# The last group's output tiles stored by column halves, in an attention and MoE kernel on one Trainium2 core

## The chip, the cores and the metric

The kernel runs on one core of one Trainium2 chip. The metric is the device time of one execution, in microseconds. A core has five engines that run their own instruction streams in order: PE (TensorE, the matrix products), DVE (VectorE), ACT (ScalarE), POOL (GpSimd) and SP (SyncE, here used for DMA only). They wait for one another through semaphores. Data lie in SBUF; PE writes its products to PSUM, 128 partitions of eight banks, from which DVE or ACT copy them out. DMAs are issued by SP, ACT or POOL, each with a queue of its own.

## What is computed

The reference does two attentions and then a feed-forward layer, on 8 batches of 8 heads, 576 tokens and 64 columns of a head; p is a pack of 32 rows for each batch and head.

```python
def sm_attn(qq, kk, vv):
    s = scale * np.matmul(qq, kk.transpose(0, 1, 3, 2))
    s = s - np.max(s, axis=-1, keepdims=True)
    a = np.exp(s)
    a = a / (np.sum(a, axis=-1, keepdims=True) + 1e-09)
    return np.matmul(a, vv)
p_packed = sm_attn(p, k, v)
x = sm_attn(q, p_packed, p_packed)      # as 4608 tokens x 512
h = x @ w_in                            # 512 x 2048
r = np.maximum(h, 0.0)
out = (r * r) @ w_out                   # 2048 x 512
```

Inputs and the output are float32; the products inside are of bfloat16 with float32 sums. The output is 4608 x 512, 9.4 MB.

## The kernel before, in words

**Work and stages.** For each of the eight batches, the first attention's scores are made (`s1_mm`, L736, or `x1_mm`), their maximum taken (`s1_max`, L755), the exponential e (`s1_exp`, L763), its transposes on PE (`s1_tr`, L769, five into one PSUM bank for each of two halves of the heads), a copy of them out (`s1_out`, through `cast`, L609 on ACT or L611 on DVE), and the product with v (`pv_mm`, L783). The result pp is normed (`pp_norm`, L792), transposed (`ppT_mm`, L802) and copied to ppT (`ppT_out`). The packed rows are then multiplied by w_in first (`m_mm`, L813; the product is called M, and copied out by `m_out` or, for batch 0, in two halves by `m_half`), and the second attention's weights, called a, are multiplied by M (`f1_mm`, L887, or `fh_mm`, L915, for parts of the first two batches). Its relu (r_b) and square give gT (`f1_relu`, `f1_sq`, `fh_relu`, `fh_sq`), the transposed input of the last product.

**The last product.** The 36 output tiles are 128 tokens by 512 columns. Twelve are made plainly, by 16 products over 2048 (`f2_mm`, L941), copied to o_sb (`f2_out`) and stored (`store`, L953). One of them, tile 31 (called TZ), is made in column halves (`fz_mm`, L959, `fz_out`). The other 24 stand in six groups of four tiles, `GROUPS` = 2 to 7, each a 2 x 2 block matrix product by seven half-size products instead of eight: sums of w_out and gT (`w_sum`, L986, `g_sum`, L993), the products (`gp_mm`, L1008), and copies and additions (`g_copy`, `g_add`, L1028) into the four quadrants (i, j) of the group's output, where i is a pair of tiles and j a half of the columns. The pieces of these are called GC.0 to GC.6; GC.2 finishes quadrant (0, 0), GC.6 (0, 1), GC.4 (1, 1) and GC.5 (1, 0).

**What sets the order.** The work is cut into pieces, each with its engine or a choice of engines, a duration, what it needs, the units that it takes (PSUM banks or pairs of banks, buffers of r_b, tiles of o_sb) and those that it frees. `Plan.forward` walks through time and starts, whenever an engine is free, the ready piece of the best priority: a level from the code plus a number from the long table `TABLE`. The instructions are then emitted in that order, under `tc.manual_schedule()`, so that each engine's stream is that of the plan. The waits between engines are not written in the kernel: they are derived, when it is built, from which instruction reads or writes which tile.

**PSUM.** One tile, `ps` (L595), holds all eight banks. `half(n)` (L600) is a bank of it, `pair(u)` (L603) two neighbouring ones. Banks 0 to 5 are taken as three pairs or, for the transposes, PV and the first plain tiles, singly (4 and 5, with 6 and 7); the outputs of the last product use banks 6 and 7 later on.

**Stores around the change** (L1303 to L1312). A group's tile needs both column halves: i = 0 waits for GC.2 and GC.6, i = 1 for GC.4 and GC.5. The tiles of the last group (those past TZ) are stored in two pieces of 64 tokens by 512 columns, 128 KB each, on whichever of SP, ACT or POOL the plan finds first (`store_any`, L1272). Tile 31 is stored in four pieces of 64 KB.

Of the kernel before, what the change touches and what calls it, by code (L numbers as in the profile page):

```python
# [14 lines left out]
P = 128  # L15
# [26 lines left out]
class Plan:  # L42
# [185 lines left out]
TABLE = {'o': {'Lk.0.0i': -36.900503, 'Lk.0.1i': 0.41924, 'Lk.0.0': -16.56608, 'LP.0': 169.009326, 'Lk.0.1':  # L228
# [292 lines left out]
def kernel_impl(tc, q, k, v, p, w_in, w_out, out):  # L521
# [23 lines left out]
    with ExitStack() as ctx:  # L545
# [45 lines left out]
        o_sb = consts.tile([P, NO, NE], F32, name="o_sb")  # L591
        still = consts.tile([P, 4], BF16, name="still")
        zero = o_sb[:, 0, :P].bitcast(BF16)

        ps = psum.tile([P, 8, 512], F32, name="ps")  # L595

        V, A = nc.vector, nc.scalar
# [802 lines left out]
```

## Time and profile before

| | |
|---|---|
| median of 3 runs | 234.08 us |
| lowest and highest | 233.74 and 234.46 us |
| the profiled execution | 233.42 us |
| its span in the trace | 231.7 us |
| mean granted clock of PE | 0.994 |
| HBM read and written | 37.22 MB and 9.44 MB |

The span goes from the first to the last event that the profiler recorded for the core, and the execution's own time is a little longer. Busy time is that of an engine's computing instructions. Matmuls are pipelined, so that neighbours overlap. In the rows below, `PEld` is PE's loading of the stationary operand, `SPq` and `ACTq` are the queues on which those engines issue DMAs, L and a number is a line of the kernel, and `out<-in` names tiles without their buffer numbers. A bracket at the end of a row is the idle time of the engine just before, and what ended it.

### The profile page before, as it was taken

To read this page: it belongs to the slowest core of one execution; us is meant where nothing else is said; L and a number is where in the kernel's file an instruction comes from. 1 tells how busy PE (TensorE), PEld (TensorE's weight loads), DVE (VectorE), ACT (ScalarE), POOL (GpSimd) and SP (SyncE) were. 2 spreads that over 40 slices of the span, in tenths; PEclk is the share of its full clock that TensorE was granted. 3 is DMA by queue.
4 is the path that set the end of the run, shared out by engine and by line. 5 is a ranking of instruction groups with operands and counts; after the bars stand their busy time and mean duration, and the time that the engine had idled before them with its cause. 6 is when DMAs were issued, how large, how long until landed. Compare 5 with 4: busy or idle time off the path is not lost.

```text
span 231.7 us, 6374 instructions
## 1 busy us (share of the span) xinstructions
PE 220.0 (95%) x2613; PEld 160.0 (69%) x2630; DVE 199.4 (86%) x336; ACT 148.4 (64%) x243; POOL 60.5 (26%) x108
## 2 busy tenths in 40 slices
PE   8978899999999999999999999999999999999991
PEld 5655664456654476768777877787668888888880
DVE  3679978999989999999999899999999997958340
ACT  3324994268955899775997936859988988310100
POOL 9787646333243575640000000000000000000010
PEclk9999999999999999999999999999999999999997
DMA  7999999999999999999999659757041001515325
GB/s 235 188 161 180 184 204 205 203 193 251 241 229 223 223 219 195 158 148 126 177 193 166 135 94 207 149 83 172 0 96 43 4 0 35 113 36 114 70 52 174
DMA packets 46668, 34.06 MB, mean 147 GB/s; under 512 B 25376, under 2 KB 38368, under 8 KB 46640
## 3 DMA queue, kind: packets, MB, share of 16 engines
q0 software_dynamic: 19488, 18.09, 50.5%
q1 hardware_dynamic: 26304, 14.98, 31.4%
q10 hardware_dynamic: 848, 0.59, 0.9%
q8 instruction: 20, 0.33, 0.6%
q14 instruction: 8, 0.07, 0.1%
HBM read 37.22 MB, written 9.44 MB: 201 GB/s over the span
## 4 chain that ended last, share of the span: by engine, by line
PE 83%; DVE 6%; DMA 5%; POOL 1%; issue 1%; ACT 1%; DVEq 0%; ACTq 0%; POOLq 0%
PE ps L1008 32%; PE ps L887 21%; PE ps L941 15%; PE ps L915 4%; PE ps L813 3%; DMA v_b<-in_v_dram 3%; DMA kq_b<-in_q_dram 2%; PE ps L959 2%; DVE gT L935 1%; PE ps L783 1%; PE ps L830 1%; PE ps L736 1%; PE ps L769 1%; POOL v_b L624 1%; DVE qT L700 1%
## 5 line engine op out<-in xcount | busy, mean ns | idle before, releaser
L897 ACT ACTIVATE r_b<-ps 128x576 bf16<-128x576 f32 x86 | 50.4, 663 | 10.1 <-PE ps L887 9.7
L887 PE MATMUL ps<-a,M 128*128 128x288 bf16 x384 | 52.3, 286 | 0.2 <-issue 0.2
L887 PEld LDWEIGHTS <-M 128*128 128x128 bf16 x384 | 37.3, 98 | 11.1 <-issue 0.2
L941 PE MATMUL ps<-w_out_b,gT 128*128 128x512 bf16 x159 | 41.3, 380 | 1.1 <-issue 0.6
L1008 PEld LDWEIGHTS <-gT 128*128 128x128 bf16 x384 | 36.9, 98 | 7.3 <-issue 1.3
L609 ACT CAST M<-ps 128x1024 bf16<-128x1024 f32 (+1 forms) x30 | 26.9, 933 | 12.4 <-PE ps L813 12.3
L609 ACT COPY o_sb<-ps 128x512 f32<-128x512 f32 (+1 forms) x23 | 12.9, 568 | 32.2 <-PE ps L1008 18.4
L1008 PEld LDWEIGHTS <-gS 128*128 128x128 bf16 x288 | 27.8, 98 | 4.5 <-issue 0.7
L953 POOL DMA_DIRECT2D out_dram<-o_sb x3 | 1.7, 556 | 108.8 <-ACT o_sb L609 103.6
L1028 DVE TENSOR_TENSOR o_sb<-o_sb,ps 128x512 f32<-128x512 f32 x30 | 20.3, 676 | 10.1 <-PE ps L1008 10.0
L907 DVE TENSOR_TENSOR gT<-r_b 128x1152 bf16<-128x1152 bf16 x37 | 27.1, 746 | 1.6 <-ACT r_b L897 1.6
L941 PEld LDWEIGHTS <-gT 128*128 128x128 bf16 x176 | 16.2, 98 | 15.4 <-issue 2.1
L1008 PE MATMUL ps<-wS,gT 128*128 128x256 bf16 x192 | 24.0, 273 | 0.0
L1008 PE MATMUL ps<-w_out_b,gT 128*128 128x256 bf16 x192 | 23.5, 273 | 0.0
L1008 PE MATMUL ps<-wS,gS 128*128 128x256 bf16 x192 | 23.3, 273 | 0.0
L923 ACT ACTIVATE r_b<-ps 128x512 bf16<-128x512 f32 (+2 forms) x30 | 17.8, 659 | 4.8 <-PE ps L915 4.7
L915 PE MATMUL ps<-a,M 128*128 128x256 bf16 (+3 forms) x160 | 18.3, 262 | 2.2 <-DVE a L878 1.0
L915 PEld LDWEIGHTS <-M 128*128 128x128 bf16 x160 | 14.0, 97 | 6.8 <-issue 2.2
L763 ACT ACTIVATE e<-ps,n 128x576 bf16<-128x576 f32 x16 | 11.7, 737 | 7.8 <-DVE n L755 7.6
L615 PE MATMUL ps<-o_sb 128*128 128x256 bf16 x89 | 13.9, 319 | 1.1 <-DVE o_sb L618 1.1
L755 DVE TENSOR_REDUCE n<-ps 128x1 f32<-128x576 f32 x16 | 11.6, 748 | 3.1 <-PE ps L736 3.0
L864 ACT ACTIVATE e<-s 128x1152 bf16<-128x1152 f32 (+4 forms) x11 | 10.0, 912 | 6.2 <-DVE s L861 6.1
(77 smaller groups left out, 322.0 us busy)
## 6 DMA issues: line engine op xcount, KB each, us to landing
out_dram<-o_sb SPq DMA_DIRECT2D x65, 128.0 KB, 3.5
kq_b<-in_k_dram POOLq DMA_DIRECT2D x14, 288.0 KB, 11.1
kq_b<-in_q_dram POOLq DMA_DIRECT2D x10, 288.0 KB, 8.7
w_in_b<-in_moe_w_in_dram POOLq DMA_DIRECT2D x16, 128.0 KB, 5.7
w_out_b<-in_moe_w_out_dram POOLq DMA_DIRECT2D x8, 256.0 KB, 9.6
v_b<-in_v_dram POOLq DMA_DIRECT2D x5, 320.0 KB, 11.8
v_b<-in_v_dram POOLq DMA_DIRECT2D x12, 128.0 KB, 8.7
v_b<-in_v_dram POOLq DMA_DIRECT2D x5, 256.0 KB, 12.2
```

The lines of the kernel that those rows point to most:

```text
L609: nc.scalar.copy(dst, src)
L615: nc.tensor.matmul(half(7)[:, :2 * P], lhsT=zero[:, :P], rhs=zero, start=True, stop=True)
L755: nc.vector.tensor_reduce(n1[b % 2][:, qd:qd + 1], ps1[b, qd], axis=AX.XY if b in XBAR else AX.X, op=ALU.max, negate=True)
L763: nc.scalar.activation(e_out(qd) if b in XBAR else e1[:, qd, :S], ps1[b, qd], ACT.Exp, bias=n1[b % 2][:, qd:qd + 1], accum_out=d1[b % 2][: ...
L887: nc.tensor.matmul(t[:, c], lhsT=M[b % 2][:, qd, fb * FB:(fb + 1) * FB], rhs=a2[b % 2][:, qd, c * HALF:(c + 1) * HALF], start=(qd == 0), s ...
L897: nc.scalar.activation(dst, src, ACT.Relu)
L907: eng.tensor_tensor(out=dst, in0=r, in1=r, op=ALU.mult)
L915: nc.tensor.matmul(t[:, c, m * w:(m + 1) * w], lhsT=M[b % 2][:, qd, fb * FB:(fb + 1) * FB], rhs=a2[b % 2][:, qd, o:o + w], start=(qd == 0) ...
L923: nc.scalar.activation(dst, ph["h", b, x, j], ACT.Relu)
L941: nc.tensor.matmul(po[t], lhsT=gT[:, fb, n0:n0 + P], rhs=w_out_b[:, fb, :], start=(fb == 0), stop=(fb == NFB - 1))
L1008: nc.tensor.matmul(pz[g, k][:, i], lhsT=a[:, f, i * P:(i + 1) * P], rhs=w[:, f], start=(k not in ON and h == 0 and f == 0 and i == 0), sto ...
L1028: nc.vector.tensor_tensor(out=oC(g, i, j), in0=oC(g, *src), in1=pz[g, z], op=ALU.add)
```

## The change

It touches three places.

First, PSUM is declared as five tiles instead of one: three of two banks and two of one bank. `half` and `pair` give the same banks as before, and `pair` may only take the pairs (0, 1), (2, 3) and (4, 5).

Second, the stores of the last group's tiles. Each quadrant (i, j) of the group has its own four stores (two tiles, two pieces of 64 tokens), of 256 columns and 64 KB, and each needs only the piece that finishes that quadrant. There are 16 instead of eight. Earlier groups are stored as before.

Third, the table of priorities is replaced by another, with keys for the new stores. (The table's lines are left out here.)

```diff
-TABLE = {'o': {'Lk.0.0i': -36.900503, 'Lk.0.1i': 0.41924, 'Lk.0.0': -16.56608, 'LP.0': 169.009326, 'Lk.0.1':
...
-        ps = psum.tile([P, 8, 512], F32, name="ps")
+        ps = [psum.tile([P, 2, 512], F32, name=f"ps{i}") for i in range(3)]
+        ps += [psum.tile([P, 512], F32, name=f"pb{i}") for i in range(6, 8)]

         def half(n):
-            return ps[:, n, :]
+            return ps[n // 2][:, n % 2, :] if n < 6 else ps[n - 3][:]

         def pair(u):
-            assert u[1] == u[0] + 1 and u[1] < 8
-            return ps[:, u[0]:u[0] + 2]
+            assert u[1] == u[0] + 1 and u[0] in (0, 2, 4)
+            return ps[u[0] // 2]
...
-                ps1[b, qd] = pair(u).rearrange("p c n -> p (c n)")[:, :S]
+                ps1[b, qd] = pair(u)[:].rearrange("p c n -> p (c n)")[:, :S]
...
-            for i in range(2):
+            for i, j, z in ((0, 0, 2), (0, 1, 6), (1, 1, 4), (1, 0, 5)) if first(g) > TZ else ():
+                for x in range(2):
+                    t = first(g) + 2 * i + x
+                    for part in range(2):
+                        add(f"ST.{t}.{j}{part}", store_any(t, (part,), slice(HN * j, HN * j + HN)), [f"GC.{z}.{g}"], free=[(f"GC.{1 - i}.{g}", 0)], lag=2.0, level=L)
+            for i in range(2 if first(g) <= TZ else 0):
                 for x in range(2):
                     t = first(g) + 2 * i + x
                     done, held = [f"GC.2.{g}", f"GC.6.{g}"] if i == 0 else [f"GC.4.{g}", f"GC.5.{g}"], [(f"GC.{1 - i}.{g}", 0)]
```

More of the change, by code (lines that the diff above doesn't have):

```diff
@@ L226 @@
 XTURN = (5, 6, 7)
-TABLE = {'o': {'Lk.0.0i': -36.900503, 'Lk.0.1i': 0.41924, 'Lk.0.0': -16.56608, 'LP.0': 169.009326, 'Lk.0.1':
[290 rows of a table removed]
+TABLE = {'o': {'Lk.0.0i': -36.900503175, 'Lk.0.1i': 0.419239945, 'Lk.0.0': -16.566079593, 'LP.0': 169.009325645,
[331 rows of a table added]
 def kernel_impl(tc, q, k, v, p, w_in, w_out, out):
```

621 rows, old and new, of the table TABLE are left out of this document.

## The prediction

> **What bounds the kernel now.** I read the page's head and chain first, then busy time by windows, then the engines' timelines at places that a comparison of the two kernels as built pointed to. The first four rows are the span, the busy line, the chain by engine, and one row of the windows (columns: window, length, then busy time of PE, PEld, DVE, ACT and POOL, granted clock, DMA share, GB/s).
>
> ```profile
> span 231.7 us, 6374 instructions
> PE 220.0 (95%) x2613; PEld 160.0 (69%) x2630; DVE 199.4 (86%) x336; ACT 148.4 (64%) x243; POOL 60.5 (26%) x108
> PE 83%; DVE 6%; DMA 5%; POOL 1%; issue 1%; ACT 1%; DVEq 0%; ACTq 0%; POOLq 0%
> 32.00:226.60 194.60, 192.90 (x2276) 140.84 (x2273) 175.69 (x277) 131.07 (x212) 36.69 (x64) 1.00 0.80 140
> ```
>
> PE is on 83% of the chain. Between 32 and 226.6 us it idles 194.60 - 192.90 = 1.70 us in all, at full granted clock. So two things follow: whatever makes PE wait in that stretch moves the end by nearly that much, because at most 1.70 us of idle time is there to swallow it; and after PE's last product only a short tail is left, which is where the stores of the change stand.
>
> The tail: additions and copies that finish output tiles, three rows of store issues among them (SPq, ACTq), the windows row of the 2 us behind PE's end, and the last three are rows of DMA issues (count, KB each, us from issue to landing), the first of them from 219 to 222 us, the other two from 226.9 us on.
>
> ```profile
> 216.19 0.58 ACT L609 COPY o_sb<-ps 128x512 f32<-128x512 f32 x1 [11.64 <-PE ps L1008]
> 221.49 0.69 DVE L1028 TENSOR_TENSOR o_sb<-o_sb,ps 128x512 f32<-128x512 f32 x1 [1.12 <-PE ps L1008]
> 223.18 0.69 DVE L1028 TENSOR_TENSOR o_sb<-o_sb,ps 128x512 f32<-128x512 f32 x1 [1.00 <-PE ps L1008]
> 223.89 3.71 SPq L953 DMA_DIRECT2D out_dram<-o_sb  x4
> 223.90 2.36 ACTq L953 DMA_DIRECT2D out_dram<-o_sb  x3
> 224.92 0.69 DVE L1028 TENSOR_TENSOR o_sb<-o_sb,ps 128x512 f32<-128x512 f32 x1 [1.06 <-PE ps L1008]
> 226.67 0.37 ACT L609 COPY o_sb<-ps 128x256 f32<-128x256 f32 x1 [7.44 <-PE ps L959]
> 227.07 0.56 ACTq L953 DMA_DIRECT2D out_dram<-o_sb  x1
> 226.70:228.70 2.00, 0.00 (x0) 0.00 (x0) 0.00 (x0) 0.34 (x1) 0.00 (x0) 1.00 0.95 270
> out_dram<-o_sb SPq DMA_DIRECT2D x1, 64.0 KB, 2.0
> out_dram<-o_sb SPq DMA_DIRECT2D x1, 64.0 KB, 3.2
> out_dram<-o_sb ACTq DMA_DIRECT2D x1, 64.0 KB, 3.4
> ```
>
> The last half tile is copied at 226.67 and stored from 227.07. Its 64 KB land 3.4 us later, at 230.5, and the span ends 1.2 us after that. The same size took 2.0 us at 219 to 222 us. The difference is the queue ahead: the last group's eight 128 KB stores (1 MB) are issued only from 223.89, when full rows are ready, and the engines that carry them are 95% busy at 270 GB/s until 228.7.
>
> **The change, part by part.** Comparing the kernels as built: PE's 5262 instructions are the same in the same order on the same PSUM banks, and DVE's are the same with one more at the end. The new table of priorities thus changes no order ahead of the last stores. Three things differ.
>
> *1. Stores, 8 of 128 KB become 16 of 64 KB.* Each quadrant's four stores now wait for its own copy or addition alone. These end at 216.19 + 0.58 = 216.8, 221.49 + 0.69 = 222.2, 223.18 + 0.69 = 223.9 and 224.92 + 0.69 = 225.6, so each sends 256 KB, the last two 1.7 us apart. That is 150 GB/s against the 270 GB/s that the window shows possible, so the queue in front of the last tile's stores is nearly empty when these start at 227.1: the last quadrant's 256 KB need 256/270 = about 0.95 us from some 0.5 us after 225.6 on. The issues don't block: three on ACT's queue took 2.36 us, 0.79 each, and the 20 of the tail from 216.8 on go over three queues (9 on ACT, 6 on SP, 5 on POOL). ACT has only the last tile's first copy between them, and that copy is off PE's path. The last tile's second half is copied by DVE instead of ACT, priced as the 0.37 us row. What the landing will be: not under 2.0 us (the row with no queue), not over 3.4 (as now), nearest to the first since the queue is gone. I take 2.0 to 2.4, middle 2.35 for two stores at once, so **-1.05 us**; ends 0 and -1.4.
>
> The Trainium skill, "DMA: Bandwidth & Descriptors", in its section "Measured (HBM→SBUF, 128 partitions, SWDGE, issued from GpSimd)", speaks against halving stores: batch transfers to 1 MiB or more, since those under 64 KB are dominated by descriptors. By its "Anatomy of one DMA" (about 2.0 us fixed plus bytes over 436 GB/s) a lone 64 KB store would be an estimated 2.15 us, near the traced 2.0. By the rule as a limit on rate there would be no gain, which is the third rival below.
>
> *2. PSUM, one tile of eight banks becomes three tiles of two banks and two of one.* No instruction moves. But the waits in the program are derived from tiles, and the builds differ in about 25 of them, all ahead of 83 us: two accesses to different banks of one pair, which were independent, are now ordered. Most of those end before the engine gets there. These do not:
>
> ```
> place   instruction that waits anew            for (its rows below)
> A 24    DVE's copy of half of M                ACT's copy of the other half
>   27    the same, for the next columns         ACT's copy
> B 35    DVE's first copy of e                  all 10 transposes, not its own 5
>   35.8  PE's next L941 product                 DVE's second copy of e as well
>   38    DVE's copy of ppT                      one more L941 product
>   38.1  PE's next L941 product                 that copy of ppT
> C 50    ACT's copy of one o_sb tile            three more L941 products
>         PE's next L941 product                 that copy
> D 67    PE's second set of transposes          ACT's copy of the first set
> E 74    ACT's copy of e                        DVE's copy of e
> F 81    ACT's copy of ppT                      DVE's copy of e
> ```
>
> Place A. Rows are start, length, engine, line.
>
> ```profile
> 24.25 0.63 DVE L611 CAST M<-ps 128x512 bf16<-128x512 f32 x1
> 24.16 0.57 ACT L609 CAST M<-ps 128x512 bf16<-128x512 f32 x1
> 27.19 0.62 ACT L609 CAST M<-ps 128x512 bf16<-128x512 f32 x1
> 27.52 0.68 DVE L611 CAST M<-ps 128x512 bf16<-128x512 f32 x1
> 28.26 0.93 PE L915 MATMUL ps<-a,M 128*128 128x256 bf16 x7 [0.28 <-DVE M L611]
> ```
>
> DVE's 24.25 now starts at 24.16 + 0.57 = 24.73, plus a hop of some 0.05 between engines (in place B, DVE's 38.07 starts 0.04 behind the end of PE's 37.81): +0.53. DVE is busy without a gap from there to the copy at 27.52, whose own new wait, to 27.19 + 0.62 = 27.81, is later by 0.3 only and so is covered by the first; if ACT is late too, it adds a little. PE's product at 28.26 waits for that copy already. Total **+0.55**.
>
> Place B.
>
> ```profile
> 34.70 0.72 PE L769 MATMUL ps<-ident,e 128*128 128x128 bf16 x10
> 35.18 0.89 DVE L611 COPY e<-ps 128x640 bf16<-128x640 bf16 x2 [0.38 <-PE ps L769]
> 35.78 0.60 PE L941 MATMUL ps<-w_out_b,gT 128*128 128x512 bf16 x2
> 36.30 0.49 PE L783 MATMUL ps<-v_b,e 128*32 128x64 bf16 x40
> 37.81 0.22 PE L802 MATMUL ps<-ident,pp 128*128 128x128 bf16 x1
> 38.07 0.23 DVE L611 COPY ppT<-ps 128x128 bf16<-128x128 bf16 x1 [0.37 <-PE ps L802]
> 37.87 0.81 PE L941 MATMUL ps<-w_out_b,gT 128*128 128x512 bf16 x3
> 38.61 0.63 PE L813 MATMUL ps<-w_in_b,ppT 64*32 64x512 bf16 x16
> ```
>
> Ten transposes take 0.72, so five more delay DVE's copies by about 0.28: they end at 35.18 + 0.89 + 0.28 = 36.35, and PE's 35.78 starts at 36.40, **+0.62**. Of the three products from 37.87 (0.81 for three, 0.216 apart as in place C, so 0.38 long), DVE's copy of ppT, 38.07, now waits for the first, to 37.87 + 0.38 = 38.25 and the hop: it ends at 38.53. The second product, at 38.09, waits for that copy: **+0.5**. L813 at 38.61 stands behind both, so +1.1 in all.
>
> Places C and D.
>
> ```profile
> 48.84 1.89 PE L941 MATMUL ps<-w_out_b,gT 128*128 128x512 bf16 x8
> 49.73 1.62 ACT L609 COPY o_sb<-ps 128x512 f32<-128x512 f32 x3
> 50.57 0.27 PE L915 MATMUL ps<-a,M 128*128 128x256 bf16 x1
> 66.61 0.69 ACT L609 COPY e<-ps 128x640 bf16<-128x640 bf16 x1
> 66.85 0.44 PE L769 MATMUL ps<-ident,e 128*128 128x128 bf16 x5
> ```
>
> C: eight products from 48.84 to 50.57 are 0.216 apart, so the sixth starts at 49.92 and ends at 50.30. ACT's first copy, at 49.73, waited for the third and now waits for the sixth: 50.35. One copy is about 0.58 (as the row at 216.19), so it ends at 50.93, and the seventh product (50.14) waits for it: **+0.85**. Queued behind on ACT are the two other copies, which come no later than the products that they need. D: ACT's copy ends at 67.30, and PE's transposes at 66.85 wait for it: **+0.5**.
>
> Places E and F.
>
> ```profile
> 74.14 0.48 DVE L611 COPY e<-ps 128x640 bf16<-128x640 bf16 x1
> 74.34 0.71 ACT L609 COPY e<-ps 128x640 bf16<-128x640 bf16 x1
> 75.35 0.53 PE L783 MATMUL ps<-v_b,e 128*32 128x64 bf16 x40
> 80.46 0.49 DVE L611 COPY e<-ps 128x640 bf16<-128x640 bf16 x1
> 80.75 0.30 ACT L609 COPY ppT<-ps 128x128 bf16<-128x128 bf16 x1
> 81.08 0.63 PE L813 MATMUL ps<-w_in_b,ppT 64*32 64x512 bf16 x16
> ```
>
> E: ACT starts at 74.66 instead of 74.34 and ends at 75.37, 0.05 past what PE's 75.35 allows. F: ACT goes from 80.75 to 81.0 and ends at 81.3, and PE's 81.08 waits for it, +0.2. Together **+0.25**.
>
> Sum: 0.55 + 1.1 + 0.85 + 0.5 + 0.25 = 3.25 us. Each of them delays DVE or PE, and the other follows, since each waits for the other's work; DVE's 175.69 us busy in the window of 194.60 leave it no room to run ahead. Of PE's 1.70 us idle some may swallow a part, and I take 0.25: **+3.0**. Bounds: 0, if no new wait ends last, and 3.4, with nothing swallowed and the second wait of A added.
>
> *3. The table of priorities* costs nothing, as no order follows from it but that of the last stores.
>
> Total: +3.0 - 1.05 = +1.95 us on the profiled execution, which took 233.42 (span 231.7 and 1.7 around it): 235.4. That execution lies 0.66 below the median of 234.08 and just under the lowest run (233.74), so I apply the difference to the median: **236.0 us**.
>
> **Rivals.**
>
> (a) *Only the tail counts.* If banks of one pair did not wait for each other after all, or the new waits ended early, part 2 is 0 and the time 234.08 - 1.05 = 233.0. For it: the reads and writes concern different banks. Against it: the waits are in the program, and the rows put the awaited end behind the waiter's start by 0.3 to 0.6 us at six places. The Trainium skill, "PSUM — Partial Sum Buffer", section "PSUM bank collisions raise a hardware error", says that two engines on different banks run clean, so the chip needs none of these waits; an engine held by a semaphore is held all the same. Chance 0.07.
>
> (b) *Half is swallowed.* A delay of one engine is made good by work ready elsewhere: the waits of B overlap with each other and PE's idle time takes a whole 1.0 to 1.7 us. Then part 2 is 1.5 to 2.0 and the time 234.5 to 235.0. Against it: PE's order is fixed, so nothing ready can be taken first. Chance 0.14.
>
> (c) *No gain at the end.* Sixteen smaller stores keep the queue as long as eight large ones (rows of 1 KB instead of 2 KB, 0.79 us an issue), and the last landing stays at 3.4 us: +3.0 to +3.2, 237.1 to 237.3. It decides if 64 KB stores move under 150 GB/s; the 270 GB/s of the window was with larger ones for the most part. Chance 0.1. All of the change's cost would then be seen, the other side of (a).
>
> **How the numbers follow.** Forecast 0.69, (a) 0.07, (b) 0.14, (c) 0.10. The forecast's own range is 235.2 to 236.9, from the swallowed part (0 to 0.7) and the landing (2.0 to 2.6). To hold 8 in 10 it reaches into (b) and to (c): 234.5 to 237.2. About 0.3% (0.7 us) is what a measurement of this kernel can tell from no change: (a) is faster, the lowest part of (b) is within it, the rest slower. So faster 0.07, same 0.06, slower 0.87.
>
> **What would show it.** After, up to PE's end: idle time ahead of PE's L941, L769 and L813 products (at their shifted lines), released by DVE's or ACT's copies of e, ppT and o_sb, of 0.3 to 0.9 us at the six places; PE's last product 3 us later than now; and a stretch from 83 us to that product as long as before. At the end: the last stores landing 2.0 to 2.4 us after their issue, and the way from PE's last product to the end of the span 1 us shorter. I am wrong if PE's last product ends as early as before (a), or if the last landing still takes over 3 us (c).

## The result, and the profile after

The changed kernel took 236.68 us (median of 6 runs, 236.10 to 237.32) against 233.93 for the kernel before (6 runs, 233.66 to 234.56): a ratio of 1.0112, 95% interval [1.0088, 1.0135], or 2.1 to 3.2 us slower. (Ratios here and below are of the mean times of the runs, so they differ a little from the quotients of the medians.) The forecast was 236.0 in a range of 234.5 to 237.2.

The profiled execution of the changed kernel took 236.94 us. Its span, busy line and chain by engine:

```profile
span 235.2 us, 6386 instructions
PE 220.5 (94%) x2613; PEld 159.8 (68%) x2630; DVE 200.7 (85%) x337; ACT 148.4 (63%) x242; POOL 61.3 (26%) x110
PE 80%; DVE 7%; DMA 6%; ACT 3%; issue 1%; POOL 1%; ACTq 0%; DVEq 0%; POOLq 0%
```

No engine's work has grown by what the span has (3.5 us): PE has 220.5 us against 220.0, DVE 200.7 against 199.4, ACT 148.4 in both. The chain is what changed: ACT stands on it with 3% instead of 1%, DVE with 7% instead of 6%. That points to a loss by waiting. The page's averages don't say where; the timelines of PE, DVE and ACT do. Lines of the kernel are 41 further down (L941 is now L982), and PSUM's banks 6 and 7 are called `pb`. Place A, from ACT's, DVE's and PE's timelines:

```profile
25.27 0.57 ACT L650 CAST M<-ps 128x512 bf16<-128x512 f32 x1
25.87 0.69 DVE L652 CAST M<-ps 128x512 bf16<-128x512 f32 x1 [0.43 <-ACT M L650]
26.62 0.75 PE L956 MATMUL ps<-a,M 128*128 128x192 bf16 x7 [0.50 <-DVE M L652]
30.04 1.14 PE L956 MATMUL ps<-a,M 128*128 128x256 bf16 x9 [0.56 <-DVE M L652]
```

The brackets are the thing to read. DVE's copy of M started beside ACT's before, and now sits idle 0.43 us until ACT's copy is over; PE then idles 0.50 us for DVE. Place B, on the same three engines:

```profile
36.52 0.72 PE L810 MATMUL ps<-ident,e 128*128 128x128 bf16 x10
37.28 0.89 DVE L652 COPY e<-ps 128x640 bf16<-128x640 bf16 x2 [0.66 <-PE ps L810]
38.23 0.59 PE L982 MATMUL ps<-w_out_b,gT 128*128 128x512 bf16 x2 [0.45 <-DVE e L652]
40.31 0.38 PE L982 MATMUL ps<-w_out_b,gT 128*128 128x512 bf16 x1
40.73 0.22 DVE L652 COPY ppT<-ps 128x128 bf16<-128x128 bf16 x1 [0.55 <-PE ps L982]
41.01 0.59 PE L982 MATMUL ps<-w_out_b,gT 128*128 128x512 bf16 x2 [0.32 <-DVE ppT L652]
41.53 0.63 PE L854 MATMUL ps<-w_in_b,ppT 64*32 64x512 bf16 x16
```

DVE waits for the end of all ten transposes (36.52 + 0.72 = 37.24), and the three products that ran without a gap from 37.87 are now one and two, with DVE's copy of ppT between them: PE to DVE to PE, where nothing in the data asks for it. Places C and D:

```profile
53.04 0.58 ACT L650 COPY o_sb<-ps 128x512 f32<-128x512 f32 x1 [0.29 <-PE ps L982]
53.67 0.81 PE L982 MATMUL ps<-w_out_b,gT 128*128 128x512 bf16 x3 [0.67 <-ACT o_sb L650]
54.32 1.36 PE L956 MATMUL ps<-a,M 128*128 128x256 bf16 x11
70.36 0.69 ACT L650 COPY e<-ps 128x640 bf16<-128x640 bf16 x1
71.11 0.44 PE L810 MATMUL ps<-ident,e 128*128 128x128 bf16 x5 [0.35 <-ACT e L650]
```

The idle time of PE in gaps of over 0.15 us, by line and what ended it (us in total, times, longest), for the kernel before from 32 to 226.6 us, and then for the changed kernel from 33.8 to 231 (the same stretch of work):

```profile
PE ps L941 <- issue: 0.6, 4, 0.2
PE ps L887 <- issue: 0.2, 1, 0.2
```

```profile
PE ps L982 <- ACT o_sb L650: 0.7, 1, 0.7
PE pb L982 <- issue: 0.6, 4, 0.2
PE ps L982 <- DVE e L652: 0.5, 1, 0.5
PE ps L810 <- ACT e L650: 0.3, 1, 0.3
PE ps L982 <- DVE ppT L652: 0.3, 1, 0.3
PE ps L928 <- ACT M L650: 0.2, 1, 0.2
```

The kernel before has five such gaps, and in none of them does PE wait for another engine. The same five are there after (the L928 row is the one at L887, put down to ACT's copy of M this time). The other four rows are new: C's, B's two, and D's.

Places E and F, and PE's next group behind them:

```profile
78.40 0.48 DVE L652 COPY e<-ps 128x640 bf16<-128x640 bf16 x1
78.96 0.69 ACT L650 COPY e<-ps 128x640 bf16<-128x640 bf16 x1 [0.25 <-DVE e L652]
84.72 0.48 DVE L652 COPY e<-ps 128x640 bf16<-128x640 bf16 x1
85.23 0.27 ACT L650 COPY ppT<-ps 128x128 bf16<-128x128 bf16 x1
85.95 0.49 PE L824 MATMUL pb<-v_b,e 128*32 128x64 bf16 x40
```

The same PE group stood at 81.63 before. The tail, by the timelines: PE's last products, the last copy, ACT's stores.

```profile
229.12 1.91 PE L1000 MATMUL pb<-w_out_b,gT 128*128 128x256 bf16 x16
231.07 0.42 DVE L652 COPY o_sb<-pb 128x256 f32<-128x256 f32 x1 [1.06 <-PE pb L1000]
226.60 5.55 ACTq L994 DMA_DIRECT2D out_dram<-o_sb  x7
```

The 2 us behind PE's end by windows (columns as in the prediction):

```profile
231.10:233.10 2.00, 0.00 (x0) 0.00 (x0) 0.39 (x1) 0.00 (x0) 0.00 (x0) 1.00 0.69 170
```

And the DMA issues from 231.3 us on, with KB each and us to landing:

```profile
out_dram<-o_sb ACTq DMA_DIRECT2D x2, 64.0 KB, 2.3
out_dram<-o_sb SPq DMA_DIRECT2D x1, 64.0 KB, 2.0
```

Behind PE's end the engines of the DMAs are 69% busy instead of 95%, and the last stores land 2.0 to 2.3 us after their issue instead of 3.2 to 3.4. So the change does what it says, and at the same time something else, which costs more.

One part of these two traces is no part of the change. PE's second set of L830 products (L871 after) waits for DVE's transpose of q, and that for q's load:

```profile
18.28 0.58 PE L871 MATMUL ps<-qT,pq 32*32 32x192 bf16 x28 [1.67 <-DVE qT L741]
```

It started at 17.18 us before. The experiments show that this start varies from run to run, in the kernel before too; so below each trace is measured from there.

### The profile page after: what moved, and what is told of

It is laid out like the page before. It is cut to its first block, busy times and chain, and to the rows that moved or that the text cites. A ratio compares the mean times of both kernels' runs of the same rounds, so it can differ in the third digit from the quotient of the medians.

```text
span 235.2 us, 6386 instructions
## 1 busy us (share of the span) xinstructions
PE 220.5 (94%) x2613; PEld 159.8 (68%) x2630; DVE 200.7 (85%) x337; ACT 148.4 (63%) x242; POOL 61.3 (26%) x110
## 4 chain that ended last, share of the span: by engine, by line
PE 80%; DVE 7%; DMA 6%; ACT 3%; issue 1%; POOL 1%; ACTq 0%; DVEq 0%; POOLq 0%
PE pb L1049 32%; PE ps L928 20%; PE pb L982 11%; PE ps L956 4%; PE ps L854 3%; PE ps L982 3%; DMA v_b<-in_v_dram 3%; DMA kq_b<-in_q_dram 3%; PE pb L1000 1%; DVE gT L976 1%; PE ps L777 1%; PE ps L871 1%; PE ps L810 1%; PE ps L824 1%; ACT r_b L964 1%
## 5 line engine op out<-in xcount | busy, mean ns | idle before, releaser
L928 PE MATMUL ps<-a,M 128*128 128x288 bf16 x384 | 52.3, 286 | 0.2 <-ACT M L650 0.2
L928 PEld LDWEIGHTS <-M 128*128 128x128 bf16 x384 | 37.3, 98 | 11.2 <-issue 0.4
L982 PE MATMUL pb<-w_out_b,gT 128*128 128x512 bf16 x128 | 34.6, 379 | 1.1 <-issue 0.6
L994 POOL DMA_DIRECT2D out_dram<-o_sb x5 | 2.7, 547 | 109.1 <-ACT o_sb L650 104.3
L1069 DVE TENSOR_TENSOR o_sb<-o_sb,pb 128x512 f32<-128x512 f32 x30 | 20.3, 677 | 10.1 <-PE pb L1049 10.0
L982 PEld LDWEIGHTS <-gT 128*128 128x128 bf16 x176 | 16.2, 98 | 17.3 <-issue 4.3
L650 ACT COPY o_sb<-pb 128x512 f32<-128x512 f32 (+1 forms) x20 | 11.5, 575 | 24.8 <-PE pb L1049 18.4
L1049 PE MATMUL pb<-wS,gT 128*128 128x256 bf16 x192 | 24.0, 273 | 0.0
L1049 PE MATMUL pb<-w_out_b,gT 128*128 128x256 bf16 x192 | 23.5, 273 | 0.0
L1049 PE MATMUL pb<-wS,gS 128*128 128x256 bf16 x192 | 23.3, 273 | 0.0
L656 PE MATMUL pb<-o_sb 128*128 128x256 bf16 x89 | 13.7, 315 | 1.1 <-DVE o_sb L659 1.1
```

Of the source, the lines that this page charges most:

```text
L650: nc.scalar.copy(dst, src)
L656: nc.tensor.matmul(half(7)[:, :2 * P], lhsT=zero[:, :P], rhs=zero, start=True, stop=True)
L928: nc.tensor.matmul(t[:, c], lhsT=M[b % 2][:, qd, fb * FB:(fb + 1) * FB], rhs=a2[b % 2][:, qd, c * HALF:(c + 1) * HALF], start=(qd == 0), s ...
L982: nc.tensor.matmul(po[t], lhsT=gT[:, fb, n0:n0 + P], rhs=w_out_b[:, fb, :], start=(fb == 0), stop=(fb == NFB - 1))
L1049: nc.tensor.matmul(pz[g, k][:, i], lhsT=a[:, f, i * P:(i + 1) * P], rhs=w[:, f], start=(k not in ON and h == 0 and f == 0 and i == 0), sto ...
L1069: nc.vector.tensor_tensor(out=oC(g, i, j), in0=oC(g, *src), in1=pz[g, z], op=ALU.add)
```

## The experiments

**The theories.** Mine: the change is two things, half stores that save about 0.9 us at the end, and a new cut of PSUM that adds waits worth 3.2 us. Rival 1: the loss is partly the later load of q, and the change brings that with it. Rival 2: the stores themselves cost. The table has, for every trace, the start of the second set of L830 products, the start of PE's last 16 products, the stretch between the two, and the time from the end of those products (1.91 us) to the end of the span.

| kernel | L830 set | last products | stretch | to the end | median against before | ratio, 95% interval |
|---|---|---|---|---|---|---|
| before | 17.18 | 224.72 | 207.54 | 5.1 | | |
| before, again | 17.24 | 224.79 | 207.55 | 4.9 | 233.69, 233.65 | 0.9999 [0.9976, 1.0022] |
| before, third trace | 17.52 | 225.08 | 207.56 | 4.9 | one run | |
| before, fourth trace | 17.60 | 225.15 | 207.55 | 4.8 | one run | |
| changed | 18.28 | 229.12 | 210.84 | 4.2 | 236.68, 233.93 | 1.0112 [1.0088, 1.0135] |
| changed, second trace | 17.45 | 228.29 | 210.84 | 4.1 | one run | |
| changed, third trace | 17.56 | 228.54 | 210.98 | 4.1 | one run | |
| PSUM cut alone | 17.73 | 228.57 | 210.84 | 4.8 | 237.02, 233.87 | 1.0157 [1.0117, 1.0198] |
| half stores alone | 17.77 | 225.31 | 207.54 | 4.1 | 233.32, 233.87 | 0.9982 [0.9964, 1.0000] |
| half stores alone, again | 17.82 | 225.37 | 207.55 | 4.1 | 233.06, 233.87 | 0.9974 [0.9947, 1.0000] |
| and one wait | 17.72 | 226.12 | 208.40 | 4.2 | 233.89, 233.87 | 0.9996 [0.9980, 1.0011] |
| half stores, later in order | 17.43 | 224.99 | 207.56 | 4.3 | 232.99, 233.87 | 0.9974 [0.9957, 0.9990] |
| half stores, held | 17.56 | 225.11 | 207.55 | 5.2 | 234.17, 233.65 | 1.0027 [0.9996, 1.0058] |
| PSUM cut 4, 2, 1, 1 | 17.70 | 267.96 | 250.26 | 4.1 | 275.62, 233.65 | 1.1778 [1.1732, 1.1824] |

**PSUM cut alone.** The kernel before, with this and no more:

```diff
-        ps = psum.tile([P, 8, 512], F32, name="ps")
+        ps = [psum.tile([P, 2, 512], F32, name=f"ps{i}") for i in range(3)]
+        ps += [psum.tile([P, 512], F32, name=f"pb{i}") for i in range(6, 8)]
```

(`half` and `pair` as in the change.)

> The kernel before with the five PSUM tiles alone; its stores and its table of priorities as before. Theory (the added waits cost 3.2 us, the half stores bring 0.9 back): about 3.2 us slower than before, 237.1, with PE's steps back at the same six places by 0.5 to 0.9 us each, and the way from PE's last product to the end of the span 5.0 us as before. Rival 1 (the loss is partly the later load of q at 17 us, which the half stores or the table bring with them): under 2.5 us slower, with the q load as early as before. Rival 2 (the half stores are what costs): no slower than before.

Measured: 237.02 us, 3.15 above before (one of its five runs took 239.42 us, which widens the interval), and its trace has the changed kernel's stretch:

```profile
17.73 0.58 PE L831 MATMUL ps<-qT,pq 32*32 32x192 bf16 x28 [1.32 <-DVE qT L701]
228.57 1.91 PE L960 MATMUL pb<-w_out_b,gT 128*128 128x256 bf16 x16
```

228.57 - 17.73 = 210.84, as in the changed kernel to the hundredth, 3.30 more than before. The way to the end is 4.8 us, as in the other traces of before. So the cut alone makes the loss, without a new store or table; rival 2 falls.

**Half stores alone.** The changed kernel with PSUM as it was:

```diff
-        ps = [psum.tile([P, 2, 512], F32, name=f"ps{i}") for i in range(3)]
-        ps += [psum.tile([P, 512], F32, name=f"pb{i}") for i in range(6, 8)]
+        ps = psum.tile([P, 8, 512], F32, name="ps")
```

> The half stores and the new table, with PSUM as one tile of eight banks as before. Theory: 0.9 us faster than before, 233.0; PE's products at their old times, and 4.1 us instead of 5.0 from PE's last product to the end of the span. Rival 1: the q load is late here too, and the time is 0 to 1 us slower than before. Rival 2 (the half stores are what costs): 2 to 3 us slower.

> The half stores with PSUM as one tile once more, to see whether this version is faster than the kernel before: its trace says 0.8 us (0.34%), the first timing 0.9982 [0.9964, 1.0]. Theory: 0.996 to 0.998, and 207.5 us again from the second set of L830 products to the last products. Rival (the gain of the tail is lost elsewhere): 0.999 or more.

Measured: 233.32 and 233.06 us, both against 233.87. The first trace at its two ends, by PE's timeline, and then its last two stores, by the DMA issues:

```profile
17.77 0.58 PE L870 MATMUL ps<-qT,pq 32*32 32x192 bf16 x28 [0.92 <-DVE qT L740]
225.31 1.91 PE L999 MATMUL ps<-w_out_b,gT 128*128 128x256 bf16 x16
```

```profile
out_dram<-o_sb SPq DMA_DIRECT2D x1, 64.0 KB, 2.0
out_dram<-o_sb ACTq DMA_DIRECT2D x1, 64.0 KB, 2.2
```

The stretch is that of before, 207.54, and the way to the end that of the changed kernel. This is the version that beats both: by the traces 0.8 us faster than before (4.9 on the mean of four traces, 4.1 here), by the timings 0.55 and 0.81 us, with intervals that just reach 1.

**One wait put back.** Half stores, PSUM as one tile, and by hand the order that the cut made at place C:

```diff
+            if (t, fb) == (2, 13):
+                wait_for(f2[t, fb], out1[0])     # the 14th product of tile 2 waits for the copy of tile 1
...
+            if t == 1:
+                wait_for(got, f2[2, 12])         # that copy waits for the 13th product of tile 2
```

> The half stores with PSUM as one tile, and one pair of the added waits put back by hand, that of place C: ACT's copy of output tile 1 waits for the 13th product of tile 2, and the 14th product waits for that copy. Nothing else is ordered anew. Theory: PE's steps back by 0.85 us (to 0.95, since here the weight load waits as well) at about 50 us and nowhere else, so 233.0 + 0.9 = 233.9. Rival (PE's delays are made good later): the step is there but is gone by 226 us, 233.0.

Measured: 233.89 us. PE and ACT at place C:

```profile
50.66 1.07 ACT L652 COPY o_sb<-ps 128x512 f32<-128x512 f32 x2 [0.29 <-PE ps L983]
51.30 0.82 PE L983 MATMUL ps<-w_out_b,gT 128*128 128x512 bf16 x3 [0.68 <-ACT o_sb L652]
226.12 1.91 PE L1006 MATMUL ps<-w_out_b,gT 128*128 128x256 bf16 x16
```

The two brackets are those of the changed kernel at C (0.29 and 0.67), and the stretch is 226.12 - 17.72 = 208.40, 0.86 longer than without the wait. One wait between engines cost 0.86 us at 50 us, and 175 us later all of it was still there. The rival, that PE makes such a delay good, falls.

**Half stores later, and held.** First the order of the plan alone:

```diff
-                        add(f"ST.{t}.{j}{part}", ..., [f"GC.{z}.{g}"], ...)
+                        add(f"ST.{t}.{j}{part}", ..., [f"GC.{y}.{g}" for y in ((2, 6), (4, 5))[i]], ...)
```

> The half stores of 64 KB with PSUM as one tile, but each quadrant's stores wait for both column halves of their rows, as before: the same 16 stores, issued at the old times. Theory (the gain at the end comes from sending each half when it is ready): the last stores land about 3.2 to 3.5 us after their issue again, and the time is that of before, 233.9, or some tenths more, since ACT, SP and POOL now issue twice as many in the same stretch. Rival (the smaller size itself makes the last landing quick): 4.1 us from PE's last product to the end, 233.0.

Measured: 232.99, and 4.3 us to the end. That is the rival's number, but the run did not make the case that it was meant for. What the plan is told sets the order; the wait comes from the data that a store reads, which is its own half. So stores left at 222.5 and 224.2 as soon as they could. What it does show: the first quadrant's 256 KB needn't leave at 216.8; 5.7 us later was as good within 0.2 us. Of the three timings of half stores with PSUM as one tile and stores free to leave, this is the one whose interval, [0.9957, 0.9990], lies clear of 1. Then with the waits themselves:

```diff
+                for z in held:                   # (2, 6) or (4, 5)
+                    wait_for(d, gc[g, z])
```

> What the run with late halves was meant to be: in that run the plan's order held the stores back, but not the waits, so that four of them left at 222.5 and four at 224.2. Here each of the 16 half stores waits by hand for both column halves of its rows, so that eight leave from about 223.9 and eight from 225.6, the times of the full stores before, with PSUM as one tile. Theory (what shortens the end is that bytes leave earlier): the last stores land 3 us or more after their issue, and the way from PE's last product to the end is 4.8 us or more; 233.9. Rival (the smaller size of a store is what counts): 4.1 us to the end, 233.2.

Measured: 234.17, 0.52 above before, and 5.2 us to the end. The stores on SP's and ACT's queues and the last two of POOL by the timeline, and then the last two of SP and ACT by the DMA issues:

```profile
224.28 4.39 SPq L999 DMA_DIRECT2D out_dram<-o_sb  x7
224.29 4.74 ACTq L999 DMA_DIRECT2D out_dram<-o_sb  x7
226.30 1.06 POOL L999 DMA_DIRECT2D out_dram<-o_sb  x2 [0.66 <-DVE o_sb L1076]
```

```profile
out_dram<-o_sb SPq DMA_DIRECT2D x2, 64.0 KB, 2.6
out_dram<-o_sb ACTq DMA_DIRECT2D x2, 64.0 KB, 2.5
```

The same 16 stores of the same size, sent at the old times, lose the gain, so timing makes it, not size. But they lose it in another way than I had said: the last stores land 2.5 to 2.6 us after their issue, not 3 or more. It is the issue that is late. SP and ACT each issue seven stores in a row from 224.28 on, at 4.39/7 = 0.63 and 4.74/7 = 0.68 us, and are done only at 228.67 and 229.03, though the last data are ready at 227.5. POOL, to which the plan gave four of the 18, was done at 227.36; so the three engines together weren't at their limit, but SP and ACT were. Here smaller stores shortened the queue in front of the DMA engines and lengthened the one in front of these two.

**Chance in the start.** The kernel before against itself, and more traces of before and of the changed kernel:

> The kernel before, unchanged, against itself: a second trace of it, and the size of a difference that means nothing. If the late q load of the changed kernels (PE's second set of L830 products 0.4 to 1.3 us later than in the first trace of before) is chance, this trace has a shift there of the same size, and the ratio is within 0.3% of 1. If it is owed to the change, the shift is under 0.1 us here.

> The kernel before once more, for its trace alone. PE's second set of L830 products started at 17.18 and 17.24 us in its two traces, and at 17.4 to 18.3 us in those of seven changed kernels. If this lateness is chance in the load of q, this one starts anywhere from 17.2 to 18.3. If it is owed to the changes, at 17.2 within 0.1.

> As the other look at the kernel before: 17.2 to 18.3 us for the start of those products if chance, 17.2 within 0.1 if the changes delay them.

> The changed kernel once more, for its trace alone. If the late load of q (18.28 us in its first trace) is chance, these products start anywhere from 17.2 to 18.3; if it is owed to the change, at 17.7 to 18.3. In either case PE's steps at the six places are those of the first trace within 0.1 us each, 3.2 us in sum, and it is 4.1 us from PE's last product to the end.

> As the other look at the changed kernel: 17.2 to 18.3 us for the start of those products if chance, 17.7 to 18.3 if the change delays them; the six steps and the tail as in its first trace.

Measured: 0.9999 [0.9976, 1.0022], and the L830 set at 17.24, 17.52 and 17.60 in the three later traces of before, 17.45 and 17.56 in the two of the changed kernel. The row of the fourth trace of before, and then that of the second trace of the changed kernel:

```profile
17.60 0.58 PE L830 MATMUL ps<-qT,pq 32*32 32x192 bf16 x28 [1.15 <-DVE qT L700]
```

```profile
17.45 0.58 PE L871 MATMUL ps<-qT,pq 32*32 32x192 bf16 x28 [0.91 <-DVE qT L741]
```

The ranges overlap, so most of the 1.1 us between the first two traces is chance, and rival 1 falls in the main. That the other kernels start some tenths later on the mean (17.39 for the four traces of before, 17.70 for the ten others, 17.76 for the changed kernel's three) stays open with so few traces. Behind that point the traces of before agree within 0.02 us, and those of the changed kernel within 0.14. The steps at the places were there again in both new traces.

**PSUM cut otherwise.** The changed kernel with a tile of four banks, one of two and two of one:

```diff
-        ps = [psum.tile([P, 2, 512], F32, name=f"ps{i}") for i in range(3)]
+        ps = [psum.tile([P, 4, 512], F32, name="ps0"), psum.tile([P, 2, 512], F32, name="ps2")]
```

> The changed kernel, with PSUM cut in another way: one tile of four banks, one of two and two of one. Orders and stores as in the changed kernel. In the build, 318 instructions of PE, DVE and ACT wait otherwise than before, where the changed kernel has 48. Theory (waits between banks of one tile, and only these, make the loss): it is far slower, by some 20 to 40 us, since nearly every pair of PSUM tiles in flight among the first four banks is now ordered, with PE idle ahead of its products for copies by DVE and ACT; an estimate by moving each instruction of the trace of before behind what it newly waits for, copies and products at their old lengths, gives about 30. Rival (a small fixed cost of having several PSUM tiles, however cut): 236 to 238.

Measured: 275.62 us, 42 us slower, just outside the 20 to 40 and 1.4 times the estimate. Its two groups of most idle time (busy, mean ns, idle before, what ended it):

```profile
L928 PE MATMUL ps<-a,M 128*128 128x288 bf16 x384 | 54.4, 285 | 17.4 <-ACT r_b L938 12.4
L938 ACT ACTIVATE r_b<-ps 128x576 bf16<-128x576 f32 x86 | 51.4, 651 | 30.9 <-PE ps L928 26.6
```

The first of them in the kernel before:

```profile
L887 PE MATMUL ps<-a,M 128*128 128x288 bf16 x384 | 52.3, 286 | 0.2 <-issue 0.2
```

Products of the same length (285 ns against 286) wait 17.4 us, most of it for ACT's relu, against 0.2 before, and ACT waits for the products; the rest of the 42 us is spread over smaller groups. Two pairs of banks in one tile, meant to be filled and emptied in turn, stand in each other's way. A fixed cost of several tiles (236 to 238) is out; the loss grows with the waits between banks that share a tile of two or four. What stays open is why the builder keeps the banks of the one tile of eight apart, and not those of smaller tiles: no run here shows it.

## Why the forecast held, step by step

- **That the cut of PSUM costs, and where.** Right. The table follows PE by rows of the timelines, from one place to the next. What it is late at first, 1.10 us, is the load of q; each step is what is added.

| PE's row (line before) | before | changed | late by | step | forecast |
|---|---|---|---|---|---|
| second set, L830 | 17.18 | 18.28 | 1.10 | | |
| behind A, L915 | 28.26 | 30.04 | 1.78 | 0.68 | 0.55 |
| behind B, L813 | 38.61 | 41.53 | 2.92 | 1.14 | 1.1 |
| behind C, L915 | 50.57 | 54.32 | 3.75 | 0.83 | 0.85 |
| behind D, L769 | 66.85 | 71.11 | 4.26 | 0.51 | 0.5 |
| behind E and F, L783 | 81.63 | 85.95 | 4.32 | 0.06 | 0.25 |
| last products, L959 | 224.72 | 229.12 | 4.40 | 0.08 | 0 |

- **The first term that was mis-sized: "of PE's 1.70 us idle some may swallow a part, and I take 0.25".** None was swallowed: the stretch is 3.30 us longer (3.30 and 3.44 in its other traces), just the raw sum of 3.25, and 0.3 above the 3.0 that I took. The rows of PE's idle time show why: from 32 us on, no gap of over 0.15 us was time spent waiting for another engine, which a delay could have used up; five of 0.16 us were "issue", and the rest of the 1.70 us was in shorter ones. A came out 0.13 higher: DVE's first copy of M took 0.69 us instead of 0.63, and its second waited too, for 0.1 us (ACT's copy at 28.67 for 0.59 ends at 29.26, DVE's starts at 29.30), which stood in the bounds. (Between the two DVE was not "busy without a gap": it idled 0.22 us at 26.25 for a product of PE. That gap swallowed nothing, since PE was late as well; it is 0.24 after.) E and F were 0.2 lower: ACT's copies were late as forecast, but PE had products of its own until 79.67 (L777) and 85.46 (L982), so that it was hardly held by them.
- **The second: -1.05 us at the end.** The way from PE's last product to the end is 4.1 to 4.2 instead of 4.8 to 5.1 us: -0.8 on the means. The landing came out as said (2.0 to 2.3), but the first trace of before has the longest tail of its four, and the last copy is 0.42 on DVE instead of 0.37 on ACT. By the Trainium skill, "DMA: Bandwidth & Descriptors", section "Anatomy of one DMA", a 64 KB store issued by GpSimd, the path that the page's fit is for, is an estimated 2.15 us. The traces are near it: the last such store of POOL took 1.9 us, and those of SP and ACT 2.0 to 2.3. The rule in that page's section "Measured (HBM→SBUF, 128 partitions, SWDGE, issued from GpSimd)", to batch to 1 MiB or more, is one on rate; as a limit here it would have spoken for no gain at the end, and the half stores alone, with their 0.8 us, speak against it for this tail.
- **The sum.** 3.3 - 0.8 = +2.5 us by the traces, +2.75 by the medians, +1.95 forecast. The 0.25 between the first two is no larger than the later start that stays open (0.3). Both terms erred to the same side, by 0.3 and 0.25, so the time came out near the upper end of what the forecast's own terms allow: 234.08 + 3.4 - 0.8 = 236.7 (the 236.9 given there is 0.2 too high).
- **The rivals.** (a), that only the tail counts, is the half stores alone: 233.1 to 233.3, against the 233.0 that it was given. It fell because of what its counterargument said, that an engine held by a semaphore is held whether the chip needs it or not. (b) and (c) did not happen: no part swallowed, and a gain at the end. The 0.79 us an issue that stood in (c) has a wait for data in it: the third of those three stores left at 225.70, when its data had just been added (224.92 + 0.69 = 225.61), and took ACT 0.56 us.

The kernel before does without these waits: at 24.16 and 24.25 us ACT and DVE copy two neighbouring banks at the same time, and at 38.07 us DVE copies ppT out of one bank while PE's products from 37.87 us on write the other of its pair. The Trainium skill, "PSUM — Partial Sum Buffer", section "PSUM bank collisions raise a hardware error", says the same: two engines on different banks run clean.

## What to carry to other kernels

When a diff changes a declaration, compare what each instruction of the built program waits for, before and after, not only the order: here no instruction of PE moved, and PE lost 3.3 us. Of the waits that are new, price those whose awaited end lies behind the waiter's start. Here, on an engine that was 99% busy and whose little idle time was no waiting for others, what they held it up came out at the end in full; only E and F, which fell while PE had other products to run, came out smaller than priced. And measure the parts of a change apart: one line of this one, the cut of PSUM, hid a gain of 0.8 us behind a loss of 3.3.

## What the runs showed of the hardware

PE's idle gaps of 0.3 to 0.7 us at the places left no mark on its speed. The changed kernel's mean granted clock is 1.000. The window that holds place B shows the full granted clock, too (the column behind POOL's), and a product of 128x512 lasts 0.38 us before and after:

```profile
30.00:42.00 12.00, 10.65 (x158) 6.75 (x159) 8.65 (x21) 7.53 (x15) 6.51 (x10) 1.00 1.25 204
```

Issuing has a price of its own. In the held run SP issued a 64 KB store every 0.63 us and ACT one every 0.68, seven in a row each, and they were done 1.2 and 1.5 us after the last data were ready. In the run of the half stores alone the same 18 stores were spread over some 11 us, and the way to the end was 4.1 us instead of 5.2.

The start differs from run to run by more than some changes are worth: q's load moved PE's 17 us mark between 17.18 and 18.28 over 14 traces. The 207.5 us behind it repeated within 0.02 us in the eight traces of kernels with PSUM as one tile and no wait added on PE.
